# Attention's fixed orders over four units, with weighted sums that cross units' borders

## The chip, the cores and the metric

The kernel runs on one core of a Trainium2 chip. Five engines work beside each other: TensorE (PE in the profile, its weight loads PEld), VectorE (DVE), ScalarE (ACT), GpSimd (POOL), and SyncE (SP), which here only issues transfers. The metric is the time of one execution on the device in microseconds, the median of several runs. Lower is better.

## The reference, cut to what matters

One transformer block over 2048 positions of width 512, all in fp32: attention with 32 heads of 16, then a gated MLP with a product over positions. The change touches only the attention.

```python
q, k, v = qkv[0], qkv[1], qkv[2]             # 32 heads, 2048 positions, 16 columns
scores = jnp.einsum("bhqd,bhkd->bhqk", q, k) * scale
p = _softmax(scores, axis=-1)
o = jnp.einsum("bhqk,bhkd->bhqd", p, v)
```

## The kernel before

Heads go in eight groups of four (HG), queries in four blocks of 512 (NQ), keys in sixteen blocks of 128 (NB). A *unit* is one group, one block of queries and one block of keys; there are 512 of them. The 16 units of one group and one query block, here called a *q block*, add into one PSUM bank, pv. The loop over n in `block_kernel` plays the units, two by two or four by four, in orders that are written out as strings; the last 22 units have an order of their own (FINAL).

For a unit there are four score products S, one for each head: keys times queries into one PSUM bank of 128 x 512 (`product`, L728), of which ScalarE takes the exponential into the tile pt (`exp`, L732). Two heads' operands (a, `t` = 0) lie on the upper partitions and two (b, `t` = 1) on the lower ones, so that an a and a b product can run on TensorE side by side. `weigh` (L754) then multiplies the exponentials with the values: four products, one for each head, each into 32 partitions of pv. It is called for a range of columns. pt has four buffers.

The exponential needs a row maximum. It is brought into S through two further rows of the query operand, qst: the rows hold minus the maximum, in a high and a low part, and meet ones in the key operand. So qst must be complete, these rows included, before the first S of its q block. The maxima are computed ahead by `max_pair`: one *pair* covers a 128-query chunk of two heads on either half, eight pairs make a q block, and LEAD = 11 pairs are done before the loop. A pair has four products M (lower half) and two m (upper half), each reduced by VectorE (L243), one v (upper half; `minus`, ScalarE's relu at L248) and one u (upper half; `plus`, VectorE at L252). When a q block's last pair is done, `end` (the letter N) reduces the parts on VectorE (L256) and splits them on GpSimd (L103, L106), and `max_rows` (the letter T) transposes them on VectorE (L282) and issues eight transfers on SP (L286) into the two rows of qst. A list `pending` lets N run only one `play` after the pair was put in line.

The letters in an order: S, M, m, v, u as above, the last digit telling which of the seven score banks to take, counted from the one longest unused; h weighs half a unit (256 columns), V a whole one; G copies the finished pv out (ScalarE, L764) and issues eight transfers on SP (L775, L777); T is as above, and inverts the sums if there are no rows to turn; f fills pv at the start. Each engine and each queue takes its work in the order in which the program issues it.

In a q block before the change, FIRST_TWO plays four units, then ORDER five times two units, then LAST two units. For the q block's maxima, N and T fall into the ORDER that starts at its eleventh unit. The sums are inverted (`invert`, L701, and four transfers) in a T or after the play that starts at its seventh unit.

## Time and profile before

| | |
|---|---|
| median of 3 runs | 1796.41 us (1796.34 to 1796.47) |
| span of the profiled execution | 1795.9 us |
| TensorE busy | 1787.7 us, 13307 matmuls |
| VectorE busy | 1522.6 us |
| ScalarE busy | 1376.8 us |
| GpSimd busy | 223.9 us |
| one q block, from 692.82 to 730.04 us | 37.22 us |

The profile is of one execution of its own, so its span and the median of the runs differ a little. A row of a timeline gives the start, the length, the engine, the line, the operation, what it writes and reads, and how many instructions were merged. In a stretch table each engine has its busy time and its count of instructions; behind them stand the granted clock of TensorE, the share of the DMA engines, and GB/s. The end of a matmul is modelled, so that starts tell more than lengths do. Attention's loop lasts from about 168 to 1287 us.

### The profile page before, as it was taken

How to read it: one execution, taken by the hardware profiler on the slowest of the kernel's cores; microseconds unless marked ns; L12 is line 12 of the kernel's file. 1: busy time of each engine (PE TensorE's matmuls, PEld its weight loads, DVE VectorE, ACT ScalarE, POOL GpSimd, SP SyncE). 2: the span in 40 equal slices, each digit the busy share in tenths (PEclk: the TensorE clock that was granted, in tenths of full speed). 3: DMA queues.
4: the chain of work that ended last, by engine and by line, in shares of the span. 5: the costliest groups of instructions: out<-in, count | busy, mean ns of one | idle time of the engine just before them, and what ended most of it. 6: DMA issues, size and time to landing. Idle time of an engine off the chain costs nothing.

```text
span 1795.9 us, 36016 instructions
## 1 busy us (share of the span) xinstructions
PE 1787.7 (100%) x13307; PEld 1045.1 (58%) x13307; DVE 1522.6 (85%) x3051; ACT 1376.8 (77%) x2673; POOL 223.9 (12%) x299
## 2 busy tenths in 40 slices
PE   9999999999999999999999999999999999999999
PEld 6876444444444444444444444444448889999998
DVE  6487999999999999999999999999947887878664
ACT  3224999999999999999999999999994444334231
POOL 2241000011010100000000000000101865001111
PEclk9999999999999999999999999999999999999999
DMA  6687221231121221022112012111137775768562
GB/s 196 182 197 191 46 31 29 52 60 34 40 57 24 52 49 28 19 52 43 19 39 46 20 40 44 29 17 20 43 92 193 212 222 182 230 210 278 182 195 91
DMA packets 251608, 169.86 MB, mean 95 GB/s; under 512 B 158264, under 2 KB 196680, under 8 KB 250088
## 3 DMA queue, kind: packets, MB, share of 16 engines
q1 hardware_dynamic: 245880, 155.09, 34.0%
q10 hardware_dynamic: 5520, 12.46, 1.9%
q8 instruction: 105, 1.72, 0.4%
q14 instruction: 71, 0.58, 0.1%
q0 software_dynamic: 32, 0.01, 0.0%
HBM read 103.88 MB, written 62.69 MB: 93 GB/s over the span
## 4 chain that ended last, share of the span: by engine, by line
PE 98%; DVE 1%; ACT 0%; DMA 0%; issue 0%; ACTq 0%; DVEq 0%
PE pv L754 30%; PE s L728 10%; PE s L238 9%; PE m L728 9%; PE m L238 7%; PE acc L109 5%; PE acc L111 5%; PE acc L110 5%; PE g L111 4%; PE g L110 4%; PE g L109 4%; PE acc L642 2%; PE tp L1369 1%; PE h L642 1%; PE acc L1390 0%; PE tp L392 0%
## 5 line engine op out<-in xcount | busy, mean ns | idle before, releaser
L732 ACT ACTIVATE pt<-s 128x512 f32<-128x512 f32 (+1 forms) x1149 | 667.7, 631 | 3.4 <-PE s L728 1.8
L754 PE MATMUL pv<-pt,vst 128*32 128x256 f32 (+1 forms) x6048 | 595.2, 467 | 0.0
L243 DVE TENSOR_REDUCE mx<-s 128x1 f32<-128x512 f32 x826 | 539.6, 682 | 42.1 <-PE s L238 35.4
L732 ACT ACTIVATE pt<-m 128x512 f32<-128x512 f32 x855 | 499.7, 615 | 0.2 <-PE s L238 0.2
L243 DVE TENSOR_REDUCE mx<-m 128x1 f32<-128x512 f32 x682 | 452.3, 682 | 28.4 <-PE m L238 22.4
L728 PE MATMUL s<-qst,kst 50*128 50x512 f32 x1193 | 418.1, 437 | 0.0
L238 PE MATMUL s<-kst,qst 48*128 48x512 f32 x963 | 344.0, 421 | 0.0
L728 PE MATMUL m<-qst,kst 50*128 50x512 f32 x855 | 340.1, 440 | 0.0
L238 PE MATMUL m<-kst,qst 48*128 48x512 f32 x794 | 291.1, 423 | 0.0
L728 PEld LDWEIGHTS s<-qst,kst 50*128 50x128 f32 x1193 | 187.3, 184 | 145.1 <-DVE mx L243 91.0
L754 PEld LDWEIGHTS pv<-pt,vst 128*32 128x32 f32 x6048 | 120.4, 108 | 217.2 <-issue 208.1
L728 PEld LDWEIGHTS m<-qst,kst 50*128 50x128 f32 x855 | 146.2, 184 | 129.3 <-DVE mx L243 88.9
L238 PEld LDWEIGHTS s<-kst,qst 48*128 48x128 f32 x963 | 166.9, 184 | 40.1 <-issue 12.8
L238 PEld LDWEIGHTS m<-kst,qst 48*128 48x128 f32 x794 | 137.1, 184 | 41.6 <-issue 15.2
L103 POOL CAST mparts<-nm 128x16 fp32r<-128x16 f32 x32 | 6.3, 198 | 866.2 <-DVE nm L256 866.2
L248 ACT ACTIVATE ab<-s 128x512 f32<-128x512 f32 x167 | 100.5, 602 | 14.1
L252 DVE CUSTOM_DVE_ANT_0 ab<-s,ab 128x512 f32<-128x512 f32 x137 | 93.1, 680 | 5.1 <-PE s L238 5.1
L994 ACT ACTIVATE ws<-a 128x512 fp32r<-128x512 f32 x78 | 44.6, 621 | 49.4 <-PE g L111 26.6
L252 DVE CUSTOM_DVE_ANT_0 ab<-m,ab 128x512 f32<-128x512 f32 x112 | 76.2, 680 | 4.8 <-PE m L238 4.8
L238 PE MATMUL s<-dst,qst 48*128 48x512 f32 x167 | 79.7, 477 | 0.0
L1064 ACT ACTIVATE z<-acc 128x464 f32<-128x464 f32 (+2 forms) x64 | 27.4, 456 | 60.0 <-PE acc L111 51.2
L111 PE MATMUL acc<-wi,hT 128*128 128x464 f32 (+2 forms) x196 | 72.0, 367 | 0.5 <-DVE hT L106 0.5
(221 smaller groups left out, 2601.0 us busy)
## 6 DMA issues: line engine op xcount, KB each, us to landing
a<-in_w_sp SPq DMA_DIRECT2D x76, 256.0 KB
qst<-q_scr SPq DMA_DIRECT2D x192, 64.0 KB
z_scr<-z ACTq DMA_DIRECT2D x32, 344.0 KB
kst<-k_scr SPq DMA_DIRECT2D x42, 256.0 KB
k_scr<-part SPq DMA_DIRECT2D x16, 512.0 KB
q_scr<-part SPq DMA_DIRECT2D x16, 512.0 KB
z<-z_scr SPq DMA_DIRECT2D x14, 344.0 KB
b<-z_scr SPq DMA_DIRECT2D x24, 172.0 KB
```

Source lines behind the costliest of these rows:

```text
L109: nc.tensor.matmul(ps, lh, rh, start=first, stop=False)
L110: nc.tensor.matmul(ps, lh, rl, start=False, stop=False)
L111: nc.tensor.matmul(ps, ll, rh, start=False, stop=last)
L238: nc.tensor.matmul(acc, q[r, p, c], keys[r, p], start=True, stop=True)
L243: nc.vector.reduce_max(at(t, e if t else e - 1), acc, axis=AX.X)
L248: nc.scalar.activation(ab[0], acc, AF.Relu)
L252: nc.vector.tensor_tensor_reduce(ab[0], acc, ab[0], 1.0, LOW, ALU.add, ALU.max, at(0, 0))
L642: yield nc.tensor.matmul(acc, o2[b][:, d, :], wo2[a][:, d, :], start=i == 0, stop=i == 3 * DB - 1)
L728: nc.tensor.matmul(out, kst[hg % 2][r, p, kb * P:(kb + 1) * P], qst[hg * NQ + qb][r, p, :], start=True, stop=True)
L732: nc.scalar.activation(out, scores, AF.Exp, scale=DH ** -0.5)
L754: nc.tensor.matmul(pv[0][32 * j:32 * j + 32, cols], vst[hg % 2][:, c:c + 32], pt[:, places[t, p], cols], start=kb == 0, stop=kb == NB - 1 ...
L994: nc.scalar.activation(hi, src, AF.Copy)
```

## The change

ORDER, FIRST_TWO and LAST now play four units each, and a q block is FIRST_TWO, ORDER, ORDER, LAST. The old ORDER stays, as ONE, for the third and fourth unit of the kernel alone. The letter w with a number weighs so many columns, and goes on into the next unit where one ends; h and V are the same code with 256 and 512. The first product of a q block in pv is marked as start only for the range that begins at column 0. N and T stand in LAST alone, and the new letter I, in ORDER, inverts the sums. The maxima are put in line one pair earlier in every play of four units.

```diff
-ORDER = "Sa0 M0 Sa2 M0 m1 Sb0 h Sb0 Sa0 M0 N m0 h v0 Sb1 Sa0 M0 u1 T Sb0 V".split()
+ONE = "Sa0 M0 Sa2 M0 m1 Sb0 h Sb0 Sa0 M0 N m0 h v0 Sb1 Sa0 M0 u1 T Sb0 V".split()
+ORDER = ("Sb0 m0 M0 Sa0 Sb1 Sa1 M0 w400 m0 Sb0 Sa1 M0 Sa0 Sb1 m0 w416 Sa1 M0 v0 M0 u0 I Sb1 w352 Sb0 m0 M0 "
+         "Sa0 Sb0 Sa1 w368 M0 v0 M0 u1 Sb0 Sa0 w512").split()
...
-FIRST_TWO = ("v0 M0 Sa1 M0 m1 Sb1 Sa0 h Sb0 m0 h G M0 Sa0 Sb1 Sa0 Sb0 m1 M0 V Sa0 M0 Sa3 Sb0 u0 M1 h "
-             "m0 Sb0 Sa0 M0 h v1 Sb0 Sa0 M1 u0 Sb0 V").split()
-LAST = "Sa0 M0 Sa2 M0 m1 Sb0 h m0 Sb0 v0 Sb0 h u0 M1 Sa0 M1 Sa0 Sb0 V".split()
+FIRST_TWO = ("Sa0 M1 m0 Sb1 m0 Sb1 Sa0 w512 G M0 Sa0 M1 m0 Sb1 Sa0 Sb0 w480 M0 v0 M0 m1 Sb1 Sa0 w224 M0 Sa0 "
+             "Sb0 u2 Sb0 w320 Sa1 M0 v1 M0 u0 Sb0 Sa0 w512").split()
+LAST = ("Sa0 M0 m0 Sb0 N m1 Sb1 Sa0 w384 M0 Sa0 M1 Sb0 m1 Sb0 Sa0 w416 v1 M0 T Sa1 M0 m1 Sb0 w352 Sb0 Sa0 "
+        "M0 u0 Sb0 Sa1 w384 v0 M0 Sa1 M0 u1 Sb0 w512").split()
...
-                                 pt[:, places[t, p], cols], start=kb == 0,
+                                 pt[:, places[t, p], cols], start=kb == 0 and cols.start == 0,
...
-                elif x == "h":
-                    h = waiting[0][1]
-                    weigh(*waiting[0][0], slice(256 * h, 256 * h + 256))
-                    waiting[0][1] += 1
-                    if h:
-                        done[0] = waiting.pop(0)[0][0]
-                elif x == "V":
-                    done[0] = waiting[0][0][0]
-                    weigh(*waiting.pop(0)[0])
+                elif x[0] in "whV":
+                    left = {"h": 256, "V": 512}.get(x) or int(x[1:])
+                    while left:
+                        unit, c0 = waiting[0]
+                        c1 = min(512, c0 + left)
+                        weigh(*unit, slice(c0, c1))
+                        waiting[0][1] = c1
+                        left -= c1 - c0
+                        if c1 == 512:
+                            done[0] = waiting.pop(0)[0][0]
...
-                    elif done[0] is not None and done[0][2] == 5 and sums_:
+                elif x == "I":
+                    if sums_:
                         invert()
...
-                while m < min(8 * HG * NQ, n // 2 + LEAD + 1 + (not place and n > 0)):
+                one = n < 4 or n + 2 == end
+                if not one and place % 2:
+                    order = None
+                elif one:
+                    order = START if not n else ONE if n == 2 else BEFORE
+                else:
+                    order = LAST if place == 6 else ORDER if place else FIRST_TWO
+                while m < min(8 * HG * NQ, n // 2 + LEAD + 1 + (not one)):
                     for kind, some in max_pair(m, True).items():
                         steps_of[kind].extend(some)
                     m += 1
-                if place or not n:
-                    if place != 1 or n == 2:
-                        play(START if not n else BEFORE if n + 2 == end else LAST if place == 7 else ORDER, units[n:n + 2])
-                else:
-                    play(FIRST_TWO, units[n:n + 4])
-                if kb == 6 and sums_:
-                    invert()
+                if order:
+                    play(order, units[n:n + (2 if one else 4)])
```

## Prediction

> **What bounds the kernel now.** I read the page first, then a stretch table over one repetition of the attention loop, then TensorE's own timeline.

> ```profile
> PE 98%; DVE 1%; ACT 0%; DMA 0%; issue 0%; ACTq 0%; DVEq 0%
> ```

> TensorE carries 98% of the chain that ended last. The next table is one q block of 16 units, from one copy of the sums to the next.

> ```profile
> core 0 of [0], span 1795.9 us
> core 0: us, PE busy (x) PEld busy (x) DVE busy (x) ACT busy (x) POOL busy (x), PEclk, DMA share, GB/s
> 692.82:730.04 37.22, 37.22 (x326) 16.11 (x322) 34.84 (x68) 36.52 (x74) 0.47 (x3) 1.00 0.10 20
> ```

> The q block takes 37.22 us and TensorE never rests in it, at full granted clock. A busy TensorE may still be badly filled, so I read it block by block (start, length, operation, count of instructions). A weighted sum is eight instructions, because each of its four products runs twice.

> ```profile
> 714.97 1.06 PE L754 MATMUL pv<-pt,vst 128*32 128x512 f32 x8
> 715.96 0.49 PE L728 MATMUL m<-qst,kst 50*128 50x512 f32 x1
> 715.97 0.50 PE L238 MATMUL s<-kst,qst 48*128 48x512 f32 x1
> ...
> 716.87 0.64 PE L754 MATMUL pv<-pt,vst 128*32 128x256 f32 x8
> 717.44 0.50 PE L728 MATMUL s<-qst,kst 50*128 50x512 f32 x1
> ...
> 718.12 0.64 PE L754 MATMUL pv<-pt,vst 128*32 128x256 f32 x8
> ...
> 719.59 1.06 PE L754 MATMUL pv<-pt,vst 128*32 128x512 f32 x8
> ...
> 725.21 0.50 PE L238 MATMUL s<-dst,qst 48*128 48x512 f32 x1
> ...
> 725.55 0.39 PE L728 MATMUL s<-qst,kst 50*128 50x512 f32 x1
> ...
> 726.91 0.49 PE L728 MATMUL s<-qst,kst 50*128 50x512 f32 x1
> ...
> 727.33 0.64 PE L754 MATMUL pv<-pt,vst 128*32 128x256 f32 x8
> 727.90 0.49 PE L238 MATMUL s<-kst,qst 48*128 48x512 f32 x1
> ...
> 729.02 1.06 PE L754 MATMUL pv<-pt,vst 128*32 128x512 f32 x8
> ```

> Differences of starts give the prices. A run over 256 columns takes 717.44 - 716.87 = 0.57, one over 512 takes 715.96 - 714.97 = 0.99. The end of attention shows a run over two whole units, with a change of weights at the border between them:

> ```profile
> 1336.08 1.92 PE L754 MATMUL pv<-pt,vst 128*32 128x512 f32 x16
> 1337.94 0.97 PE L728 MATMUL s<-qst,kst 50*128 50x512 f32 x6
> ```

> It takes 1.86. A column therefore costs between 0.42 / 256 = 1.64 ns and, border and all, 0.87 / 512 = 1.70; I take 1.67, which leaves 0.14 for the run itself, and 1.86 - 0.14 - 1024 x 0.00167 = 0.01 for a border. Score products start two at a time, one per half of the array (715.96 and 715.97); I call such a step a slot. A block of three slots takes 716.87 - 715.96 = 0.91, of two 0.68, of one 0.42, and the block at 727.90 (seven products, of which four use the same half, so four slots) 1.12. One round of ORDER is 719.59 - 714.97 = 4.62.

> **The change: fewer runs, more slots.** I count each fixed order by halves (Sa, m, v, u use the upper one, Sb, M the lower). ORDER for four units was twice 3, 2, 3 slots with six runs; now it is blocks of 4, 4, 3, 3, 3 slots with five runs. The weighted columns stay 2048.
> - Runs for four units: before 4 x 0.57 + 2 x 0.99 = 4.26; after 2048 x 0.00167 + 5 x 0.14 + two borders = 4.14.
> - Blocks: before 4 x 0.91 + 2 x 0.68 = 5.00; after 2 x 1.12 + 3 x 0.91 = 4.97. The block that is saved pays for the seventeenth slot.

> That is 9.26 to 9.11, a gain of 0.15. LAST (4, 4, 3, 3, 3 slots, five runs, two borders) replaces an ORDER and the old LAST at the same prices: 0.15 again. FIRST_TWO was 4, 1, 4, 3, 2, 3 slots, 5.16, and six runs, 4.26; now it is 4, 4, 3, 3, 4, 5.18, and five runs with one border, 4.13: a gain of 0.11. Its piece of 32 columns is not in the trace; beyond its columns it costs between 0 and the 0.14 of a run of its own, and I take 0.05, nearer to the border's 0.01, since it stands inside a run. A q block is one FIRST_TWO, two ORDERs and one LAST: 0.06 + 3 x 0.15 = 0.51 gained.

> **VectorE and ScalarE** have the same 68 and 74 instructions in less time. Their 34.84 and 36.52 still fit into 37.22 - 0.51 = 36.71, and ScalarE has more room than that, since its rows overlap. What can wait is a score bank. In ORDER's third block VectorE gets M, M, u and the reciprocal I. At a pitch of 0.60 each (the rows at 714.43 and 715.02, below) and 0.25 for I (706.86) it needs 2.05, while block and run last 0.91 + 0.73 = 1.64: it falls up to 0.41 behind, and the next block's products reuse those banks. Seven banks absorb some of it; no row shows how much. Bounds 0 and 0.41 in each of the two ORDERs; I take 0.10, as TensorE waits for no bank in the table above. Gain left: 0.31 a q block.

> **The step that decides: T is moved from a round of ORDER into LAST.** T turns the row maxima of the next q block (L282) and issues eight transfers on SP into two rows of that block's qst (L286). The first Sa of FIRST_TWO reads those rows, and TensorE takes its products in order, so everything behind it waits too. Before, T stands in the third ORDER of the q block (n = 10 of 16):

> ```profile
> 702.09 0.49 PE L238 MATMUL s<-kst,qst 48*128 48x512 f32 x1
> 702.65 0.69 DVE L243 TENSOR_REDUCE mx<-s 128x1 f32<-128x512 f32 x1 [0.35 <-PE s L238]
> ...
> 706.86 0.25 DVE L701 RECIPROCAL rcp<-sums 128x16 f32<-128x16 f32 x1
> ...
> 714.43 0.68 DVE L243 TENSOR_REDUCE mx<-m 128x1 f32<-128x512 f32 x1
> 715.02 0.68 DVE L243 TENSOR_REDUCE mx<-s 128x1 f32<-128x512 f32 x1
> ...
> 716.23 0.20 DVE L282 STREAM_TRANSPOSE mturned<-mparts 128x32 f32<-128x32 f32 x1
> ```
> ```profile
> 716.46 5.33 SPq L286 DMA_DIRECT2D qst<-mturned  x8
> ```
> ```profile
> 722.00:722.50 0.50, 0.50 (x8) 0.46 (x4) 0.50 (x2) 0.50 (x2) 0.00 (x0) 1.00 0.02 4
> 722.50:723.00 0.50, 0.50 (x11) 0.16 (x8) 0.50 (x2) 0.50 (x2) 0.00 (x0) 1.00 0.01 1
> 723.00:723.50 0.50, 0.50 (x10) 0.19 (x4) 0.50 (x2) 0.50 (x2) 0.00 (x0) 1.00 0.00 0
> ```

> The transpose starts at 716.23, SP needs 5.33 to issue the eight, and the stretches (last two columns: DMA share, GB/s) show packets until somewhere between 722.50 and 723.00. From transpose to last packet it is 6.27 to 6.77. The first reader is the score at 725.55, 9.32 after the transpose: at least 2.5 to spare.

> After the change T stands in LAST's third block, behind the reduction of that block's first M. From the start of that block: 0.56 until VectorE can begin on M (702.65 - 702.09), 0.60 for it (the pitch of the rows at 714.43 and 715.02), so the transpose starts 1.16 in. TensorE still has ahead of it three blocks of three slots and runs of 352, 384 and 512 columns: 3 x 0.91 + 3 x 0.14 + 1248 x 0.00167 + 0.01 = 5.24. So FIRST_TWO's first Sa is wanted 4.08 after the transpose, and the first Sb, which reads the other half of the rows, one slot (0.34, from 725.21 to 725.55) later. The rows need 6.27 to 6.77. TensorE therefore waits 6.27 - 4.42 = 1.85 to 6.77 - 4.08 = 2.69, the latter if the first Sa waits for all eight. The signal may follow the last packet by a little, and VectorE may reach T late by the 0.41 above, so I put the upper end at 3.1 and take 2.3. T can't go earlier there: N, which fills T's input, is in LAST's first block, because the last of that q block's maxima are taken in the ORDER before. Nothing covers the wait. SP, POOL and the transfers are otherwise idle then, so no queue adds to it, and what TensorE would have given ScalarE and VectorE comes later by the same amount.

> The trace here shows no landing signal, only packets. [...]

> **Sum.** The wait comes once for each of the 30 q blocks after the first: 30 x 2.3 = 69. The gain is 30 x 0.31 = 9. Net 60, so the profiled span would go from 1795.9 to 1855.9; the median of the runs, 1796.41, lies 0.5 above that span, which makes 1856. Ends: 30 x 1.85 = 55 with the gain whole (30 x 0.56 = 17, the small piece free) gives +38 or 1834; 30 x 3.1 = 93 with the gain more than lost to the banks (2 x 0.41 against 0.51, so 9 more) gives +102 or 1898, but both late ends together are unlikely: I stop at 1885.

> **Rivals.**
> 1. *The rows are not needed so soon, or arrive in time; faster.* The place is FIRST_TWO's first Sa, and it decides from 4.08 to 4.42 us between transpose and landing. Were the maxima of T those of a later q block, T could move freely. For it: in the trace before nobody is seen to wait for L282 or L286. Against it: the maxima run 11 pairs ahead, so pairs 8 to 15 are done in units 0 to 11, just before units 16 to 31 use them, and eight issues alone fill 5.33. Then only the gain is left: 1796 less 9 to 15, so 1781 to 1787.
> 2. *The issue of instructions becomes the bound; slower.* For four units there are now seven pieces, so 56 + 32 products and as many loads, 176 instead of 160. 4.62 for 80 instructions is 58 ns each; if that were a limit, 176 x 58 = 10.2 against 9.26, four times in a q block, 30 times: +113, or 1909. Against it: the products at 715.96 and 715.97 start 0.01 apart, each with its load, which a queue that gets one instruction in 58 ns and is empty could not do.
> 3. *The wait costs the clock too; slower.* If the wait let the granted clock fall to half for the next block and run, 2.1 more a q block: +63, or 1920. No row here has a TensorE gap of 2 us in the middle of work. [...]

> **How the numbers follow.** Forecast (wait of 1.8 to 3.1) 0.82; rival 1 0.11; rival 2 0.02; rival 3 0.02; 0.03 that a wait of under 0.6 just balances the gain, within 0.2% (3.6 us, about what a measurement of this kernel can tell from no change). Slower is 0.86, same 0.03, faster 0.11. The range 1832 to 1885 leaves out rival 1 and the rare ends, under 2 in 10.

> **What would show it.** Right: a TensorE gap of about 2.3 us at each start of FIRST_TWO, with the transpose about 4 us ahead of it; q blocks of about 39.2 us; ORDER rounds of four units near 9.1 to 9.3. Wrong: no gap there, or q blocks under 37.22 (rival 1); even spacing of TensorE's instructions at 58 ns and no gap (rival 2); PEclk under 1.00 (rival 3).

## The result, and the profile after

The changed kernel takes 1908.75 us (median of 5 runs, 1907.64 to 1919.55), the kernel before 1796.34 beside it (1796.28 to 1796.47). The ratio is 1.0638, with a 95% interval of 1.0619 to 1.0657: slower, by 112 us, where 60 were forecast. The profiled execution has a span of 1907.0 us.

The chain of waits of the changed kernel, shares by engine:

```profile
PE 88%; SPq 5%; DMA 3%; DVE 2%; issue 2%; ACT 0%; DVEq 0%
```

TensorE no longer carries nearly all of it. SP's issues and the transfers have 8%, VectorE 2%. The groups of waits between 200 and 1300 us (engine, tile and line, then its releaser; us in total, times, longest) say where they come in:

```profile
PE m L731 <- DMA qst<-mturned: 25.5, 13, 2.4
PE s L731 <- DMA qst<-mturned: 13.5, 7, 2.2
```

The score product (now L731) waits for the rows that T writes into qst. The timeline around one start of a q block (start, length, engine, line) shows the whole step:

```profile
690.72 0.20 DVE L285 STREAM_TRANSPOSE mturned<-mparts 128x32 f32<-128x32 f32 x1
690.95 5.31 SPq L289 DMA_DIRECT2D qst<-mturned  x8
693.86 1.07 PE L757 MATMUL pv<-pt,vst 128*32 128x512 f32 x8
696.91 0.47 PE L731 MATMUL m<-qst,kst 50*128 50x512 f32 x1 [1.99 <-issue]
698.69 1.93 PE L757 MATMUL pv<-pt,vst 128*32 128x512 f32 x8
```

The run before ends at 694.92, and the first score starts at 696.91, 6.19 after the transpose. There are 30 such gaps, one at each FIRST_TWO, of 1.81 to 2.36 us, 1.95 in the mean. For 20 of the 27 up to 1300 us the profile names these transfers; for the others, the one shown among them, it names no releaser (issue). The last row is the second surprise: a run over 512 columns is recorded with 1.93 instead of 1.07. A stretch table, cut along the clock's own windows, shows why (the column behind POOL's is the granted clock of TensorE):

```profile
core 0: us, PE busy (x) PEld busy (x) DVE busy (x) ACT busy (x) POOL busy (x), PEclk, DMA share, GB/s
690.51:693.93 3.42, 3.42 (x41) 1.78 (x44) 3.19 (x8) 3.36 (x8) 0.00 (x0) 1.00 0.03 7
693.93:697.34 3.41, 1.42 (x11) 0.38 (x11) 1.49 (x4) 1.36 (x3) 0.00 (x0) 1.00 0.02 3
697.34:700.75 3.41, 3.41 (x17) 0.93 (x16) 1.89 (x3) 2.23 (x5) 0.00 (x0) 0.50 0.28 77
700.75:704.17 3.42, 3.42 (x15) 1.16 (x15) 1.89 (x3) 2.71 (x5) 0.00 (x0) 0.50 0.10 20
704.17:707.58 3.41, 3.41 (x41) 1.80 (x39) 2.77 (x5) 2.74 (x6) 0.00 (x0) 1.00 0.15 35
```

After the gap the clock is at half for 6.83 us; 15 or 17 matmuls get through in a stretch that holds 41 at full clock. Of the 30 gaps 24 are followed by such a fall, 14 times for 3.41 us and 10 times for 6.83. All 24 falls, from 205.82 to 1393.66 us, begin on one grid of 3.413 us: they start at whole multiples of it from one another. In each of the 24 one window of the grid holds 1.71 us or more of the gap. The six gaps without a fall lie across a line of that grid, with at most 1.24 us of the gap in one window. One of them is the gap of 1.99 us at 409.42:

```profile
407.21:410.62 3.41, 2.21 (x18) 0.64 (x14) 2.47 (x6) 2.56 (x6) 0.00 (x0) 1.00 0.02 3
410.62:414.03 3.41, 2.62 (x19) 1.17 (x21) 1.89 (x3) 2.12 (x5) 0.00 (x0) 1.00 0.73 94
414.03:417.45 3.42, 3.42 (x40) 1.48 (x36) 3.14 (x6) 3.42 (x9) 1.04 (x1) 1.00 0.59 81
```

Each window has only a part of the gap, and the clock stays whole. The row that answers to the one q block shown of before (37.22 us, TensorE busy throughout) is now, from one copy of the sums to the next:

```profile
660.09:700.69 40.60, 38.61 (x346) 17.95 (x346) 35.21 (x67) 36.98 (x74) 0.46 (x3) 0.96 0.21 49
```

It takes 40.60. TensorE is idle for 1.99 of that, and its busy time, at a mean clock of 0.96, is 1.4 us longer for the same work. The q blocks lie between 40.3 and 43.4.

### The profile page after: what moved, and what is told of

It reads as the page before. It is cut to its first block, busy times and chain, and to the rows that moved or that the text cites. A ratio compares the mean times of both kernels' runs of the same rounds, so it can differ in the third digit from the quotient of the medians.

```text
span 1907.0 us, 37593 instructions
## 1 busy us (share of the span) xinstructions
PE 1840.5 (97%) x14035; PEld 1104.5 (58%) x14035; DVE 1533.3 (80%) x3051; ACT 1396.4 (73%) x2673; POOL 223.6 (12%) x299
## 4 chain that ended last, share of the span: by engine, by line
PE 88%; SPq 5%; DMA 3%; DVE 2%; issue 2%; ACT 0%; DVEq 0%
PE pv L757 25%; PE s L731 10%; PE s L241 9%; PE m L731 7%; PE m L241 6%; PE acc L112 5%; PE acc L114 5%; PE acc L113 5%; SPq L289 5%; PE g L114 4%; PE g L113 4%; PE g L112 4%; DMA qst<-mturned 3%; PE acc L645 2%; DVE mx L246 2%
## 5 line engine op out<-in xcount | busy, mean ns | idle before, releaser
L246 DVE TENSOR_REDUCE mx<-s 128x1 f32<-128x512 f32 x881 | 578.3, 683 | 87.0 <-PE s L241 37.3
L757 PE MATMUL pv<-pt,vst 128*32 128x512 f32 (+15 forms) x6776 | 598.5, 450 | 0.0
L246 DVE TENSOR_REDUCE mx<-m 128x1 f32<-128x512 f32 x627 | 418.1, 682 | 93.4 <-PE m L241 59.2
L731 PE MATMUL s<-qst,kst 50*128 50x512 f32 x1188 | 423.8, 447 | 23.6 <-DMA qst<-mturned 13.5
L241 PE MATMUL s<-kst,qst 48*128 48x512 f32 x995 | 378.2, 447 | 0.0
L731 PE MATMUL m<-qst,kst 50*128 50x512 f32 x860 | 335.7, 447 | 35.3 <-DMA qst<-mturned 29.3
L731 PEld LDWEIGHTS s<-qst,kst 50*128 50x128 f32 x1188 | 197.3, 190 | 181.9 <-ACT pt L735 98.2
L757 PEld LDWEIGHTS pv<-pt,vst 128*32 128x32 f32 x6776 | 147.0, 110 | 206.1 <-issue 184.5
L731 PEld LDWEIGHTS m<-qst,kst 50*128 50x128 f32 x860 | 158.8, 195 | 109.8 <-issue 63.7
L255 DVE CUSTOM_DVE_ANT_0 ab<-m,ab 128x512 f32<-128x512 f32 x135 | 91.9, 681 | 0.0
L251 ACT ACTIVATE ab<-s 128x512 f32<-128x512 f32 x133 | 83.4, 627 | 3.5 <-PE s L241 2.9
L251 ACT ACTIVATE ab<-m 128x512 f32<-128x512 f32 x115 | 72.1, 627 | 13.6 <-PE m L241 11.7
L255 DVE CUSTOM_DVE_ANT_0 ab<-s,ab 128x512 f32<-128x512 f32 x114 | 77.6, 681 | 0.1
```

The costliest lines, as they stand in the source:

```text
L241: nc.tensor.matmul(acc, q[r, p, c], keys[r, p], start=True, stop=True)
L246: nc.vector.reduce_max(at(t, e if t else e - 1), acc, axis=AX.X)
L251: nc.scalar.activation(ab[0], acc, AF.Relu)
L255: nc.vector.tensor_tensor_reduce(ab[0], acc, ab[0], 1.0, LOW, ALU.add, ALU.max, at(0, 0))
L731: nc.tensor.matmul(out, kst[hg % 2][r, p, kb * P:(kb + 1) * P], qst[hg * NQ + qb][r, p, :], start=True, stop=True)
L757: nc.tensor.matmul(pv[0][32 * j:32 * j + 32, cols], vst[hg % 2][:, c:c + 32], pt[:, places[t, p], cols], start=kb == 0 and cols.start == 0 ...
```

## The experiments

The theory after the result: all of the loss comes from T's new place, and it has two parts, the wait for the rows and the half clock behind it; the runs and blocks by themselves cost nothing. Rivals: the new orders are slow in themselves, or the half clock comes from something other than the wait.

| kernel | median, us | ratio to before, 95% interval | falls of the clock in the attention |
|---|---|---|---|
| changed | 1908.75 | 1.0638 (1.0619 to 1.0657) | 24 |
| T in LAST's first block | 1794.64 | 0.9989 (0.9980 to 0.9998) | 0 |
| T in LAST's second block | 1816.55 | 1.0111 (1.0095 to 1.0126) | 0 |
| changed, wait filled | 1861.50 | 1.0359 (1.0345 to 1.0374) | 1 |
| before, T late | 2015.39 | 1.1221 (1.1179 to 1.1264) | 29 |
| changed, wait filled in part | 1900.85 | 1.0585 (1.0567 to 1.0603) | 22 |
| the same, in pairs | 1876.17 | 1.0447 (1.0431 to 1.0463) | 6 |
| changed, rows from two queues | 1801.88 | 1.0036 (1.0020 to 1.0052) | 1 |
| T early, short maxima and exponentials | 1778.35 | 0.9897 (0.9883 to 0.9912) | 0 |
| before, short maxima and exponentials | 1789.38 | 0.9961 (0.9947 to 0.9975) | 0 |
| T early, other sequences | 1800.45 | 1.0022 (1.0013 to 1.0031) | 0 |

### T in LAST's first block

N goes to the head of LAST and T to the end of its first block; all else is as changed.

```diff
-LAST = ("Sa0 M0 m0 Sb0 N m1 Sb1 Sa0 w384 ... w416 v1 M0 T Sa1 M0 m1 Sb0 w352 ...
+LAST = ("N Sa0 M0 m0 Sb0 m1 T Sb1 Sa0 w384 ... w416 v1 M0 Sa1 M0 m1 Sb0 w352 ...
```

> In LAST of the changed kernel N is played first and T at the end of the first block, so that the transpose comes about 2.5 us earlier in the round and the eight transfers have 6.5 us or more before FIRST_TWO's first S. Theory (late rows make the wait of 1.8 to 2.4 us, and the wait makes the half clock): both go, no stretch under clock 1.00 in the attention, 1908.75 - 58 - 55 = about 1796; if the sum of the prediction holds for runs and slots, 1781 to 1787. Rival (TensorE's instructions are issued too slowly, 176 for four units): T's place changes little, 1900 to 1910.

Measured: 1794.64 us, faster than before by 2 us (0.9989), with no gap and no fall. One q block in a stretch table:

```profile
692.36:729.52 37.16, 37.16 (x346) 17.88 (x344) 35.22 (x68) 36.69 (x75) 0.56 (x4) 1.00 0.10 20
```

So the new runs and blocks are not slow in themselves, and T's place alone makes the loss of 114. But the gain is 2 us where the sum had 9 (the upper price 15).

### T in LAST's second block

N stands at the head of LAST again, but T in its second block, behind that block's second M.

```diff
+LAST = ("N Sa0 M0 m0 Sb0 m1 Sb1 Sa0 w384 M0 Sa0 M1 T Sb0 m1 Sb0 Sa0 w416 v1 M0 Sa1 M0 m1 Sb0 w352 ...
```

> As the run before, but T stands in LAST's second block, behind its second M: the transpose is about 1.3 us earlier than in the changed kernel. Theory: a wait of 0.6 to 0.8 us remains at each of 30 q blocks, too short to bring the clock down: 20 to 24 us above the run with T in the first block, so about 1817. If any wait at all halves the clock: 1850 or more.

Measured: 1816.55 us. The timeline at one start of a q block:

```profile
694.48 1.07 PE L757 MATMUL pv<-pt,vst 128*32 128x512 f32 x8
696.00 0.47 PE L731 MATMUL m<-qst,kst 50*128 50x512 f32 x1 [0.46 <-ACT pt L735]
```

The gap is 0.46 here, and it ends with two signals close together: a transfer's, 0.13 before the score, and that of the exponential which frees the bank, 0.04 before it (the profile names the later one). A gap of 0.37 to 0.93 us stands at every q block where the kernel with T in the first block has none, and the clock never falls. Between the two places the time goes up by 22 us, some 0.7 for each of 30 q blocks: the wait grows with the place of T, without the clock taking part.

### The wait filled

Nine products of keys with keys, which nobody reads, stand ahead of the first score of each q block. They change no output and add work for TensorE where it would wait.

```diff
                     out = bank(by_age(x[2:]))
+                    if order is FIRST_TWO and unit[2] == 0 and not places:
+                        for _ in range(DUMMY):      # DUMMY = 9
+                            nc.tensor.matmul(out, kst[unit[0] % 2][:KS, 0, :P], kst[unit[0] % 2][:KS, 0, :512],
+                                             start=True, stop=True)
                     product(out, *unit, t, p)
```

> The changed kernel, T where the change puts it; ahead of the first S of each q block nine products of key columns with key columns (48 x 512, read by nobody, into the bank that this S then writes) run on TensorE, about 2 us of work inside the wait. Theory (wait and half clock are two losses, the second caused by TensorE standing still): the 30 waits stay, the clock stays 1.00, about 1908.75 - 55 = 1854 (1848 to 1862). Rival (the clock falls for another reason, such as the burst that follows the wait): clock as in the changed kernel, 1905 or more.

Measured: 1861.5 us. The timeline at one start of a q block (eight of the nine products are in the row; the ninth starts at 678.46):

```profile
675.51 1.07 PE L758 MATMUL pv<-pt,vst 128*32 128x512 f32 x8
676.51 2.11 PE L808 MATMUL m<-kst 48*128 48x512 f32 x8
678.68 0.40 PE L732 MATMUL m<-qst,kst 50*128 50x512 f32 x1
```

TensorE is busy until the rows are there, and the first score comes 2.17 after the run. From the transpose to that score it is 6.13 us in the mean of 30 q blocks, against 6.16 in the changed kernel, so the wait is as long as before; but of 24 falls of the clock one is left. That takes the loss apart: 1861.5 - 1794.6 = 67 us is the wait (2.2 for each of 30), and 1908.8 - 1861.5 = 47 is the half clock behind 23 falls, which the products took away without shortening the wait.

The fall that is left, by the timeline and by stretches:

```profile
635.39 2.35 PE L808 MATMUL s<-kst 48*128 48x512 f32 x9
```
```profile
635.49:638.90 3.41, 3.31 (x16) 2.11 (x16) 1.20 (x4) 0.92 (x2) 0.00 (x0) 1.00 0.22 38
638.90:642.31 3.41, 3.41 (x17) 1.24 (x15) 1.56 (x3) 2.48 (x5) 0.00 (x0) 0.50 0.18 43
```

TensorE rests for only 0.1 us of the window ahead of it. So TensorE did not stand still here before the clock fell, against the theory; nearly all of the nine products lie in one window.

### The kernel before, with T late

One part of the change alone: in the orders of before, T leaves ORDER (the inversion stays there, as I, under the condition that it had) and stands behind LAST's first M.

```diff
-ORDER = "Sa0 M0 Sa2 M0 m1 Sb0 h Sb0 Sa0 M0 N m0 h v0 Sb1 Sa0 M0 u1 T Sb0 V".split()
+ORDER = "Sa0 M0 Sa2 M0 m1 Sb0 h Sb0 Sa0 M0 N m0 h v0 Sb1 Sa0 M0 u1 I Sb0 V".split()
-LAST = "Sa0 M0 Sa2 ...
+LAST = "Sa0 M0 T Sa2 ...
```

> The kernel before with one part of the change alone: T is taken out of ORDER and put behind the first M of the old LAST; its other use, the inversion, stays in ORDER. The transpose is then 3.5 to 3.9 us ahead of FIRST_TWO's first S. Theory: a wait of about 2 to 2.7 us at each q block and half clock behind it, 1796 + 60 to 80 + about 50 = 1905 to 1930. Rival (the new orders are slow by themselves, T's place matters little): 1796 to 1800.

Measured: 2015.39 us, far above what was expected. Stretches along the grid:

```profile
699.96:703.37 3.41, 0.96 (x12) 0.28 (x4) 1.66 (x3) 1.48 (x3) 0.00 (x0) 1.00 0.02 5
703.37:706.78 3.41, 3.41 (x19) 1.35 (x23) 1.40 (x3) 1.82 (x4) 0.00 (x0) 0.50 0.38 77
706.78:710.20 3.42, 3.42 (x19) 1.36 (x15) 2.22 (x4) 2.79 (x6) 0.00 (x0) 0.50 0.05 10
710.20:713.61 3.41, 3.41 (x22) 1.03 (x14) 1.56 (x3) 1.64 (x4) 0.00 (x0) 0.50 0.15 31
```

The wait (2.45 us in this q block) is what was expected; the half clock mostly lasts three to five windows instead of one or two. (The profiled execution took 2029.06 us, the longest of the four.) That T's place alone makes a loss of this kind, without the new runs, is shown. Why the clock stays down longer here is taken up below.

### The wait filled in part

The first reading of the falls was that over half of one window, some 1.8 us, must be idle. Three of the nine products leave a shorter gap.

```diff
-DUMMY = 9
+DUMMY = 3
```

> The changed kernel with three unread products of keys and keys (48 x 512) ahead of the first score of each q block, where nine filled the whole wait. They should leave a gap of TensorE of 1.2 to 1.4 us. Theory (the clock falls only after a gap of about 1.8 us or more, over half of one 3.41 us window): no fall of the granted clock, q blocks of 39.3 us, 1861 us, as with nine. Rival (the limit lies lower, between the 0.52 us of the kernel with T in LAST's second block and 1.8): most gaps are followed by half clock and the time is 1890 to 1908 us.

Measured: 1900.85 us with 22 falls. One of them, first in the timeline, then by stretches:

```profile
692.71 0.96 PE L808 MATMUL m<-kst 48*128 48x512 f32 x3
694.60 0.47 PE L732 MATMUL m<-qst,kst 50*128 50x512 f32 x1 [0.94 <-issue]
```
```profile
692.85:696.26 3.41, 2.39 (x14) 1.11 (x18) 1.55 (x4) 1.24 (x3) 0.00 (x0) 1.00 0.25 52
696.26:699.67 3.41, 3.41 (x15) 1.16 (x7) 1.87 (x4) 2.64 (x6) 0.00 (x0) 0.50 0.15 36
```

The theory falls. A gap of 0.94 is enough here, in a window in which TensorE is busy for 2.39 us; in the changed kernel the window at 407.21 had only 2.21 and was followed by full clock. So neither the gap nor the busy time decides. What differs is how full the array is: the three products use 48 of its 128 rows, with nothing beside them, like the nine in the window at 635.49.

A new theory, from these windows alone: the clock falls behind a window in which too little of the array is used. I weighted each product with its rows times columns of the 128 x 128 array (the largest form in the profile is 128*128; 0.39 for 50 x 128, 0.375 for 48 x 128, 0.25 for 128 x 32) and, in a first count, with 0.30 us for a score product and 0.46 for 512 columns of a weighted one; a limit of about 0.44 of the whole then parted the windows ahead of a fall from the others.

### The wait filled in part, in pairs

Each of the three products gets a twin on the other half of the array, which goes to the bank that M takes next and isn't read either. The gap must stay; the array is fuller before it.

```diff
+                        other = bank(ages[1])
                         for _ in range(DUMMY):
-                            nc.tensor.matmul(out, kst[unit[0] % 2][:KS, 0, :P], ...
+                            for r, to in ((slice(0, KS), out), (slice(RG, RG + KS), other)):
+                                nc.tensor.matmul(to, kst[unit[0] % 2][r, 0, :P], ...
```

> As with three unread products ahead of the first score of each q block, but each with a twin on the array's other half, started beside it: the gap should stay at 0.9 to 1.1 us, while the array is fuller in the time before it. New theory (what counts in a window of 3.41 us is the used part of the array, each product weighted by its rows and columns; below about 0.44 of the whole the next window runs at half clock): the windows that had 0.30 to 0.44 now have 0.37 to 0.54, so 4 to 6 of the 22 falls are left, and the time is 1866 to 1875 us. Rival (only the time without any product counts): some 22 falls as before and 1895 to 1907 us.

Measured: 1876.17 us with 6 falls, the upper end of the count expected and 1 us over the time. One of the q blocks without a fall, first in the timeline, then by stretches:

```profile
679.09 0.96 PE L810 MATMUL m<-kst 48*128 48x512 f32 x6
681.00 0.46 PE L732 MATMUL m<-qst,kst 50*128 50x512 f32 x1 [0.94 <-issue]
```
```profile
678.06:681.47 3.41, 2.47 (x19) 0.95 (x17) 1.59 (x4) 1.45 (x3) 0.00 (x0) 1.00 0.02 3
681.47:684.89 3.42, 3.34 (x25) 1.31 (x27) 2.81 (x5) 3.20 (x7) 0.00 (x0) 1.00 0.34 81
```

The gap is the same 0.94, and the busy time nearly so (2.47 against 2.39), but the clock stays whole. Six products where there were three, in the same time, took 16 of 22 falls away. The rival, that only time without a product counts, is out.

With a count whose lengths come from pitches in the rows (0.23 for a score product that follows another on its half, 0.43 for 512 columns of a weighted one, half of a 512-column run less its own 0.14), the 80 windows ahead of a fall between 170 and 1440 us, in five of the six traces that have falls, use 0.13 to 0.39 of the array, and the other windows at full clock, some 1610, 0.385 or more; one fall lies among the others. A window of undisturbed work has 0.67. The sixth trace, with the whole wait filled, had no part in this fit and agrees with it: the window ahead of its one fall, in which TensorE is busy for 3.31 of 3.41 us, uses 0.38, and all others 0.41 or more. Over the six traces no limit on busy time parts the same windows with fewer than 26 on the wrong side, on the number of products with fewer than 17, on the products' summed lengths with fewer than 4; with their rows and columns as weights it is 1. This is a fit, with one forecast that came out nearly; that the clock goes by rows times columns isn't shown.

### Rows from two queues

T's eight transfers are shared out between SP and GpSimd, in the changed kernel.

```diff
-                nc.sync.dma_start(
+                (nc.sync if j == 0 else nc.gpsimd).dma_start(
                     qst[g][r0:r0 + 2].bitcast(F32)...
```

> The changed kernel with four of T's eight transfers issued by GpSimd and four by SP. Theory: what is late is the issue on SP, 0.65 us for each of the eight; with four on a queue the rows land 2.6 us earlier, the wait of 1.95 us is gone, and with it the half clock: q blocks of 37.2 us, 1794 to 1800 us. Rival: GpSimd, for whose issues this case has no row, takes twice as long for one (four in 5.2 us), or the rows are late for another reason: the wait stays between 1 and 2 us and the time between 1830 and 1908 us.

Measured: 1801.88 us, 2 us over the range, with one fall. The timeline of one q block:

```profile
683.21 0.20 DVE L285 STREAM_TRANSPOSE mturned<-mparts 128x32 f32<-128x32 f32 x1
683.44 2.70 SPq L289 DMA_DIRECT2D qst<-mturned  x4
684.06 2.24 POOL L289 DMA_DIRECT2D qst<-mturned  x4 [3.40 <-DVE mx L246]
...
686.36 1.07 PE L757 MATMUL pv<-pt,vst 128*32 128x512 f32 x8
687.35 0.50 PE L731 MATMUL m<-qst,kst 50*128 50x512 f32 x1
```

Both queues are done by 686.30, and the first score follows the run without a gap, 4.14 after the transpose. So it was the issue of eight transfers by one queue that was late. One q block still waits 1.94, with a fall behind it; there SP begins at 1204.2, as usual, but GpSimd only at 1207.4:

```profile
1207.38 2.25 POOL L289 DMA_DIRECT2D qst<-mturned  x4 [5.99 <-PE s L731]
```

Why GpSimd is late there is open; that q block and its neighbours (39.6, 39.9 and 37.9 us) make up 6 of the 7 us by which this kernel lies behind the one with T early.

### Short maxima and exponentials

Where did the gain go? In the kernel with T early the runs have the predicted lengths, but some blocks are longer than their slots. ScalarE's timeline there, and TensorE's at the same time:

```profile
699.93 0.62 ACT L735 ACTIVATE pt<-s 128x512 f32<-128x512 f32 x1
700.41 0.63 ACT L735 ACTIVATE pt<-m 128x512 f32<-128x512 f32 x1
700.89 0.64 ACT L251 ACTIVATE ab<-s 128x512 f32<-128x512 f32 x1
701.37 1.75 ACT L735 ACTIVATE pt<-s 128x512 f32<-128x512 f32 x3
```
```profile
701.50 0.50 PE L731 MATMUL s<-qst,kst 50*128 50x512 f32 x1
...
702.07 0.50 PE L731 MATMUL s<-qst,kst 50*128 50x512 f32 x1
702.50 0.83 PE L757 MATMUL pv<-pt,vst 128*32 128x368 f32 x8
```

ScalarE takes one bank every 0.48 us without a rest: 74 instructions are 35.5 of a q block's 37.16. The block of three slots at 701.50, the fourth of an ORDER, lasts 1.00 instead of 0.91. The load of weights for its last product, at 702.07, stands here:

```profile
702.07 0.18 PEld L731 LDWEIGHTS s<-qst,kst 50*128 50x128 f32 x1
```

It starts only with its product, where the load before it, at 701.84, is done ahead of its own. It starts 0.04 after the exponential of 701.37 gave the bank free (at 702.03, by the semaphores in the trace), and the run comes 0.43 behind that product. Among the third and later loads of a block, between 200 and 1280 us, 154 start so within 0.07 us of ScalarE's release of a bank, and 59 of VectorE's.

To test it, ScalarE's exponentials take only 384 of a bank's 512 columns from the ninth unit on, and so do VectorE's maxima M and m of all pairs in the loop, in the kernel with T early and in the one before. The other columns of pt are set to 1 by GpSimd, so that a quarter of the exponentials and of the maxima is left out; TensorE's work is whole.

```diff
-            nc.vector.reduce_max(at(t, e if t else e - 1), acc, axis=AX.X)
+            nc.vector.reduce_max(at(t, e if t else e - 1), acc[:, :CUT] if late else acc, axis=AX.X)
...
-                    exp(pt[:, len(places), :], out)
+                    played[0] += not len(places)
+                    w = CUT if played[0] > 8 else 512      # CUT = 384
+                    if w < 512 and not places:
+                        nc.gpsimd.memset(pt[:, :, w:], 1.0)
+                    exp(pt[:, len(places), :w], out[:, :w])
```

> The kernel with T early (LAST's first block) in which, from the ninth unit on, VectorE's maxima and ScalarE's exponentials take 384 of a score bank's 512 columns; the other columns of pt are set to 1 by GpSimd. TensorE's work is all there. Theory (the gain that the sum saw and the kernel with T early lacks, 0.5 us a q block, lies in waits for score banks): q blocks of 36.7 us, about 1781 us. Rival (TensorE itself takes longer for the new blocks): q blocks stay at 37.1 to 37.2 us, about 1794 us.

> The kernel before, cut in the same way: maxima and exponentials of 384 of 512 columns from the ninth unit on, the rest of pt set to 1 by GpSimd. Theory (no wait for a bank before the change): q blocks stay at 37.2 us, about 1796 us, within 3 us. Rival (bank waits were in the old orders as well, and in like amount): q blocks of 36.7 to 36.9 us, 1781 to 1787 us, as much less as the kernel with T early loses.

Measured: 1778.35 and 1789.38 us. One q block of each in a stretch table, with T early first:

```profile
690.20:726.82 36.62, 36.62 (x349) 16.23 (x346) 29.38 (x68) 31.18 (x74) 8.82 (x19) 1.00 0.09 19
```
```profile
686.69:723.69 37.00, 37.00 (x322) 14.25 (x324) 29.69 (x67) 31.46 (x74) 9.82 (x20) 1.00 0.10 20
```

With faster consumers the new orders gain 0.54 a q block (37.16 to 36.62), a little more than expected, and the block that took 1.00 takes 0.90 (starts at 702.90 and 703.80):

```profile
702.90 0.50 PE L732 MATMUL s<-qst,kst 50*128 50x512 f32 x1
...
703.80 0.82 PE L758 MATMUL pv<-pt,vst 128*32 128x368 f32 x8
```

The late loads fall from 154 and 59 to 16 and none. The missing gain was in waits for banks. By the middle of 24 q blocks, 0.15 of it is in FIRST_TWO's last block, 0.11 in the fourth block of each ORDER and 0.09 in the fourth of LAST; the other sixteen blocks have 0.1 together. Both engines were made faster at once, so their shares aren't parted by this experiment. The orders before had such waits too, 0.2 a q block (37.22 to 37.00), which was not expected: blocks of two slots go from 0.68 to 0.70 down to 0.66. Without them on either side, the new orders are ahead by 0.38.

### Other sequences

The kernel with T early, the letters of each block set in another sequence so that banks come free more evenly; slots and number of runs are the same, the lengths of some runs are not.

```diff
-ORDER = ("Sb0 m0 M0 Sa0 Sb1 Sa1 M0 w400 m0 Sb0 Sa1 M0 Sa0 Sb1 m0 w416 Sa1 M0 v0 M0 u0 I Sb1 w352 ...
+ORDER = ("m1 Sb0 Sa0 M0 M1 Sa0 Sb0 w368 M1 Sa1 Sb0 m0 Sa1 Sb1 m0 w384 Sa3 M0 v2 M0 u0 I Sb1 w384 ...
```

> The same runs and slots as the kernel with T early, in other sequences of letters: ORDER, FIRST_TWO and LAST rewritten so that the maxima and scores reuse the score banks at a more even pace (runs of 368, 384, 384, 400 and 512 columns in ORDER). Theory (the kernel with T early loses 0.5 us a q block to bank waits, which depend on the sequence): q blocks between 36.7 and 37.0 us and 1781 to 1790 us. Rival (VectorE and ScalarE are so near their limit that any sequence waits as much): q blocks of 37.1 us or more and 1793 us or more.

Measured: 1800.45 us, slower than before by 0.2%, and q blocks of 37.4: a miss. The timeline of one block:

```profile
701.02 0.50 PE L241 MATMUL s<-kst,qst 48*128 48x512 f32 x1
...
702.26 0.86 PE L757 MATMUL pv<-pt,vst 128*32 128x144 f32 x16
```

A block of four slots takes 1.24 instead of 1.12. These sequences wait more. In this block it is for ScalarE:

```profile
701.82 0.18 PEld L731 LDWEIGHTS m<-qst,kst 50*128 50x128 f32 x1 [0.27 <-ACT pt L735]
```

Late loads as counted above are 175 for ScalarE (154 with T early) and 94 for VectorE (59).

The rival isn't shown by that: one other sequence was tried, and a better one may exist. The kernel with T early is the fastest full one found, by 0.1%.

## Why the prediction was right and wrong

**Right: the step that decides, and its mechanism.** From the run's end (694.92) back to the transpose (690.72) it is 4.20 us, where 4.08 was worked out; the rows took 6.19, where 6.27 to 6.77 was read from the packets. The gap was 1.95 in the mean, within 1.81 to 2.36, against 2.3 and bounds of 1.85 to 3.1; as a lengthening of the q block with the wait filled it is 2.2 (37.16 to 39.33 in the middle), and 30 of these are the 67 us that filling the wait left over, against 69. The mean lies near the early end because the interval of the packets was used for the landing, and the transfers were there a little before it.

**Wrong: the clock.** The step that failed is rival 3, in which the wait also halves the clock. It had a chance of 0.02 and its price was left out of the forecast and of the range; it happened behind 24 of 30 gaps, and 23 of the falls cost 47 us. Its price was sound: 2.1 for each fall, against 47 / 23 = 2.0. With 47 for the clock, 7 for the gain that was missing and 2 less for the wait, the forecast of 1856 becomes 1908, where 1908.75 was measured. What failed is the small chance. The row of the profile that was missing, a TensorE gap of 2 us in the middle of work, was taken as no evidence, and the 0.02 was the author's estimate, with no row behind it. The changed kernel shows falls on a grid of 3.413 us, and ahead of the one at 697.34 a window in which TensorE was busy for 1.42 of 3.41 us. In the trace before the clock never falls, so it could have shown neither; with no row on either side the chance should have been near an even one, and the range should have reached 1920.

**Wrong in size: the gain.** It was 0.31 a q block, 9 us, after 0.20 for waits for banks; measured 0.06, 2 us. The runs have the prices that were given (five of ORDER's runs add up to 4.14 in the kernel with T early, as worked out). The term for bank waits is the one that was mis-sized: a q block was put at 36.71 without them and 36.91 with 0.20 for them, and it takes 36.62 with short maxima and exponentials and 37.16 whole, so 0.54 where 0.20 was taken and 0.82 was the bound. In the two ORDERs, the only place that the term had, it came out as put: 0.11 each, in the block behind the third. What it left at nothing is FIRST_TWO and LAST, with 0.15 and 0.09 in one block each. The fit in ORDER is partly luck, since the term went by VectorE's arrears there, while the bank in the block shown is freed last by ScalarE. "ScalarE has more room than that, since its rows overlap" was the mistake: its rows overlap, but it starts a new one only every 0.48 us.

**Wrong in a side remark.** "T can't go earlier there": it can. N at the head of LAST and T at the end of the same block keep the order of the maxima, and the rows are then in time.

**The other rivals.** No gap, or rows in time (rival 1), did not happen in the changed kernel; where T is early there is no wait, but the 1781 to 1787 of that rival would have missed by the bank waits. The issue of instructions (rival 2) gave nearly the measured time, 1909, and is wrong all the same: the kernel with T early issues the same instructions in 1794.64 us.

**Left open.** Why the clock stays at half for three to five windows in the kernel before with T late. The count of the used array doesn't tell it. With the lengths of full clock, its windows at half clock that are followed by another such use 0.36 of the array (the middle value) and those that end a fall 0.40; in the changed kernel it is the other way round, 0.41 and 0.39.

## What to carry to other kernels

A transfer that is issued late by design should be placed by counting back from its first reader: here transpose, eight issues at 0.66 us and the landing made 6.2 us, and a few letters earlier in an order string were worth 114 us (a second queue, 107). A wait of TensorE was not priced by its length alone: behind 24 of the 30 gaps, those of which one window of 3.413 us held 1.71 us or more, the work ran at half clock, and the price went from 67 to 114 us here, and from some 66 (30 gaps of 2.2) to 219 in the old orders. Banks are handed here from TensorE to two engines that are 95% busy (VectorE 35.22 of 37.16 us, ScalarE 74 starts at 0.48), and fewer and longer pieces gained 0.06 of the 0.31 a q block that the sum had; look at the pitch of such engines' starts, not at the length of their rows.
